# Filling rows of the sorted token table: nine scatters behind each region's last row, spread over the program, in place of three plain stores early in it

## The chip, the core and the metric

The kernel runs on one core of a Trainium2 chip. The metric is the device time of one execution in microseconds (us), as the median of several runs. TensorE is called PE here (its weight loads PEld), VectorE DVE, ScalarE ACT, GpSimd POOL, and SyncE SP. SP issues nearly all plain transfers, POOL issues the transfers whose row addresses are computed on the chip (scatters).

## The reference

A retention layer feeds a mixture of experts, and every token goes to one expert.

```python
for t in range(S):                       # B 4, H 8, S 768, D 64
    state = gamma * state + k[:, :, t] (outer) v[:, :, t]
    y[:, :, t] = scale * q[:, :, t] @ state
x = y as rows of N = 3072 tokens, 512 wide
expert_idx = argmax(x @ w_gate);  gate_w = softmax weight of that expert
for e in range(8):                       # w1 512 x 1024, w2 1024 x 512
    out[mask_e] = gate_w[mask_e] * (relu(x[mask_e] @ w1[e]) @ w2[e])
```

## The kernel before

**Retention.** The sequence is cut into 24 chunks of 128 tokens (6 for each of 4 batches), and the loop `for g in range(NCH)` handles one chunk g per step. `load(g)` brings 1 MB of q, k, v of a chunk (tiles `qkv_t`, `qkv_w`), issued by SP in the order of the program. In step g PE computes the scores of chunk g + 1 (`scores`, L256, into `sp`), the part carried from the state (L285), the transposed rows of chunk g - 1 (L314, into `tr`), the state's update (L271) and the output (L295, into `Y`). DVE masks the scores (`Sb`, L259), and `sp` has two buffers, so the scores of a chunk wait until DVE has masked those of the chunk before. POOL scales v two chunks ahead (`scale`, `vs`, L245). ACT copies rows to `xrow` (L315). Between these steps stand pieces of the first expert's weights: ACT rounds a raw piece (`whi`, L136) and POOL takes the remainder (`wlo`, L137).

**Sorting.** After each group of 6 chunks DVE picks the expert of each token (`choose`, L360 to L372, up to step g = 6 for the first group), PE ranks the tokens, and POOL scatters each chunk's 128 rows of 520 floats (`send_rows`, L629) into the table `x_sorted` in DRAM. That table has nine regions of 3200 rows: expert 0 has two (region 0 for the first half of the tokens, region 8 for the second), experts 1 to 7 one each. `KEY` is the row of each token, `cnt` the number of rows in each region.

**Reading the table.** The experts' token counts are not known ahead, so every region is read to a fixed length: 256 rows of regions 0 and 8, and `CAPS` (452, 424, ... 360) rows, rounded up to a multiple of 32, of the others, which are taken in the order of their counts (`expert_at[1]` is the expert with the most tokens; SP reads these numbers into registers at L568). What is computed from rows behind a region's last row is thrown away when the results are scattered.

**Filling rows.** `prefill` puts finite numbers into rows that a region may not reach: rows 320 to 479 of regions 1 to 7 and rows 128 to 255 of regions 0 and 8, as three plain stores (L230) that SP issues behind the load of chunk 6. Their source is the first tile of q.

**Order and waits.** The order of every engine's instructions is the order of the program text (`manual_schedule`). Waits are put in by a dependency tracker: a read of `x_sorted` waits for the scatters and stores into it that come before it in the program, a scatter waits for the reads that come before it, and scatters don't wait for one another (`scatter_rows` declares that). A new tile on old memory waits for the old tile's users.

**From the last chunk to the first experts.** After step 23 POOL scatters chunks 22 and 23. SP fetches region 8 (`xg1` and `meta8`, L147, L151), then reads the experts' numbers, then fetches region `expert_at[1]` into `buf` (L147), and then the first two pieces of that expert's w1 (`raw`, L128). PE meanwhile finishes the first half of expert 0 (L671, L688) and starts on its second half: 8 blocks of the hidden layer (L804, `ph`, three buffers), and then L827. For each block ACT writes `hh` (L809) and DVE `hl` (L810), which frees `ph`. Behind block 2 and block 3 ACT and DVE each get one half of the split of expert 1's first w1 piece (`whi`, `wlo`). `send` (L695) scatters the finished rows `yo` of expert 0's first half to `out`, in two parts.

Of the kernel before, what the change touches and what calls it, by code (L numbers as in the profile page):

```python
# [9 lines left out]
F32 = mybir.dt.float32  # L10
F32R = mybir.dt.float32r
BF16 = mybir.dt.bfloat16
I32 = mybir.dt.int32
AF = mybir.ActivationFunctionType
ALU = mybir.AluOpType
AX = mybir.AxisListType

B, H, S, D = 4, 8, 768, 64
E, DM, F = 8, 512, 1024
N = B * S  # L20
P = 128
# [10 lines left out]
E1 = E - 1  # L32
E9 = E + 1
# [5 lines left out]
REG = N + P  # L39
SLICE = P + 2  # L40
ROW = 4 * SLICE
# [57 lines left out]
def retention_moe(ctx, tc, qkv, wg, w1, w2, cst, gdec, ustr, out):  # L99
    nc = tc.nc  # L100
# [5 lines left out]
    k_ = lambda name: cs[:, OFF[name][0]:OFF[name][1]]  # L106
# [5 lines left out]
    x_sorted = tc.dram_tile([E9, REG, ROW], F32, name="x_sorted")  # L112
    x_rows = x_sorted.rearrange("e n m -> (e n) m")
# [17 lines left out]
    def split(pos, part, i, engine, n=2):  # L131
        if i == 0:
            wparts[pos, part] = [wp.tile([P, 4, 512], F32R, name=n, tag="w", bufs=11) for n in ("whi", "wlo")]
        raw, (hi, lo) = raws[pos, part], wparts[pos, part]
        h = slice(n * i, n * i + n)
        nc.scalar.copy(out=hi[:, h], in_=raw[:, h])  # L136
        engine.tensor_tensor(out=lo[:, h], in0=raw[:, h], in1=hi[:, h].bitcast(F32), op=ALU.subtract)  # L137
# [20 lines left out]
    gate = pool("gate", 1)  # L158
# [7 lines left out]
    cnt = gate.tile([P, E9], F32, name="cnt")  # L166
    capv = gate.tile([P, E9], F32, name="capv")
    cnt7 = gate.tile([P, E1], F32, name="cnt7")
    metas = {c: gate.tile([P, nb, 2], F32, name=f"meta{c}") for c, nb in ((0, 2), (E, 2), (E1, 3))}
    masks = {c: gate.tile([P, nb], I32, name=f"mask{c}") for c, nb in ((0, 2), (E, 2), (E1, 3))}  # L170
    sidxs = {c: gate.tile([P, nb], I32, name=f"sidx{c}") for c, nb in ((0, 2), (E, 2), (E1, 3))}
# [6 lines left out]
    sel, se = [gate.tile([P, E1, E1], F32, name=n) for n in ("sel", "se")]  # L178
    us = gate.tile([P, P], BF16, name="us")

    s7 = lambda t: t.unsqueeze(1).broadcast_to([P, E1, E1])
# [17 lines left out]
    with ExitStack() as actx:  # L199
# [3 lines left out]
        gsm = apool("gsm", 1)  # L203
# [9 lines left out]
        qs, vss, Sbs, xTs, lgs, Ys, xrows = {}, {}, {}, {}, {}, {}, {}  # L213
# [4 lines left out]
        def load(g, part=slice(0, 4)):  # L218
            if g not in qs:
                early = AHEAD <= g < FIRST  # L220
                qs[g] = (wp.tile([P, 4, DM], F32, name="qkv_w", tag="w", bufs=11) if early else
                         ld.tile([P, 4, DM], F32, name="qkv_t", tag="ld"))
            nc.sync.dma_start(out=qs[g][:, part], in_=qkv[g][:, part])

        def prefill():

            row = qs[0].rearrange("p i m -> p (i m)")[:, 0:ROW].unsqueeze(1)
            for classes, a, n in ((slice(1, E), 320, P), (slice(1, E), 320 + P, 32), (slice(0, E9, E), P, P)):
                dst = x_sorted[classes, a:a + n].rearrange("e n m -> n e m")
                nc.sync.dma_start(out=dst, in_=row[0:n].broadcast_to(list(dst.shape)))  # L230

        def turned(g, i):
            return qs[g][:, i].rearrange("a (p t) -> a p t", p=NP)
# [84 lines left out]
        def send_rows(g):  # L318
            b, c = divmod(g, CPB)
            scatter_rows(tc, x_rows, KEY[:, g, 0:1], xrows[b][:, c].rearrange("t q m -> t (q m)"), "sorted")  # L320

        def logits(t):
            ps, tag = (ps_m, "mt") if t < NCH // 2 - 1 else (ps_1, "misc")
            L = ps.tile([P, TW], F32, name="L", tag=tag)
            for p in range(NP):
                nc.tensor.matmul(out=L[32 * p:32 * p + 32, :], lhsT=wgs[:, p, :], rhs=xTs[t][:, p, :],
                                 start=True, stop=True)
            LT = wk.tile([P, TW], F32, name="LT", bufs=1)
            nc.scalar.copy(out=LT, in_=L)
            state["LT"] = LT  # L330
# [87 lines left out]
        def fill(n, lows=True):  # L418
            for i in range(state["half"], state["half"] + n):
                hidden(i // 2, i % 2)  # L420
                if i % 2 and lows:
                    low(i // 2, nc.gpsimd)
            state["half"] += n
# [18 lines left out]
        nc.sync.dma_start(out=us32, in_=ustr)  # L442
        for g in range(3, FIRST):
            load(g)
            if g == 6:
                prefill()
            if g in (7, 10):
                fetch(0, (g - 7) // 3)
        scores(0)
# [11 lines left out]
        for g in range(NCH):  # L461
            b, c = divmod(g, CPB)
            t = g // 2
            if LATE + 1 < g < NCH - 1:
                scores(g + 1)
            if g < NCH - 1:
                carry(g)
            if g > 0:
                rows(g - 1)
            if g + 2 < NCH:  # L470
                scale(g + 2)
            if g in placed:
                s = stages[placed[g]]
                for name in ("slots", "weights", "advance", "label"):
                    s[name]()
                if g == NCH // 2 + 2:
                    s["counts"]()
            for i in range(*sends.get(g, (0, 0))):
                send_rows(i)
            for i in splits.get(g, ()):  # L480
                split(0, *i, nc.gpsimd, 1)
            if g in logits_at:
                logits(logits_at[g])
            if g == 21:
                prep_slices(nc, nc.gpsimd, xhl[:, 0], xhl[:, 1], xt0, xg0, 0, P)
            if c < CPB - 1:
                update(g)
            if g == 21:
                prep_slices(nc, nc.gpsimd, xhl[:, 0], xhl[:, 1], xt0, xg0, 4, P)
            if g == LATE + 1:  # L490
                scores(g + 1)
            if g == NCH - 1:
                token_mask(0, cnt[:, 0:1], EARLY)
                token_index(0)
                hidden, low, result, send = early_half(tc, ld.tile([P, 2, DM], F32, name="yo0", tag="ld"),
                                            wk.tile([P, 4, EARLY], F32, name="rx0", tag="xT"),
                                            wp, ps_m, wparts, xhl, sidxs[0], metas[0], out)
                stages[3]["rank"]()
                fill(FILL[0])
                carry(g)  # L500
            output(g)
            if g in ranked and g < NCH - 1:
                stages[ranked[g]]["rank"]()
            if g <= LATE:
                scores(g + 1)
            if g == 2:
                nc.vector.tensor_copy(out=us, in_=us32)
                nc.vector.tensor_scalar(out=run, in0=k_("ebase"), scalar1=1.0 / P, scalar2=None, op0=ALU.mult)
                nc.vector.tensor_copy(out=wgs[:, :, E:E + 1], in_=wgs[:, :, 0:1])
            if g in chosen:  # L510
                s = stages[chosen[g]] = gating(chosen[g])
                s["choose"]()
                s["soft"]()
            if g == 17:
                xg0 = rawp.tile([P, NJ0, SLICE], F32, name="xg0", tag="raw")
                xt0 = rawp.tile([P, KD, EARLY], F32, name="xt0", tag="raw")
                xhl = new_xhl()
            if g < AHEAD:
                load(FIRST + g)
            elif FIRST <= g < NCH - AHEAD:  # L520
                load(g + AHEAD)
            if g == 18:
                fetch_rows(xg0, 0, NJ0)
                fetch_meta(metas[0], 0, 2)
            if g in fetches:
                fetch(0, fetches[g])
# [17 lines left out]
            final[name]()  # L544
        for g in range(22, 24):
            send_rows(g)
        fill(FILL[4])
        xg1 = ld.tile([P, NJ0, SLICE], F32, name="xg1", tag="ld")
        xt1 = ld.tile([P, KD, EARLY], F32, name="xt1", tag="ld")
# [8 lines left out]
                                       op0=ALU.mult, op1=ALU.add)  # L558
        gt = sq("gt")
        nc.vector.tensor_tensor(out=gt, in0=s7(c8), in1=i7(c8), op=ALU.is_gt)  # L560
        pos = gsm.tile([P, E1], F32, name="pos")
# [6 lines left out]
            expert_at[i + 1] = nc.sync.value_load(eid7[0:1, i:i + 1], min_val=1, max_val=E - 1)  # L568
        for f in range(done, KF):
            low(f, nc.vector)  # L570
        xg = buf[:, 0:MAXB * SLICE].rearrange("p (j m) -> p j m", m=SLICE)
        fetch_rows(xg, expert_at[1], -(-CAPS[1] // 32))
        fetch(1, 0)
# [8 lines left out]
        for j, w in pieces:  # L582
            cut_slices(nc, nc.vector, xhl1[:, 0], xhl1[:, 1], xt1, j, w)
        result(1, 0)
        result(1, 1)
        send(1)
        token_mask(E, cnt[:, E:E9], EARLY)
        token_index(E)
# [6 lines left out]
                                in1=cnt7.unsqueeze(2).broadcast_to([P, E1, 16]), op=ALU.is_ge)  # L595
        nc.vector.tensor_scalar(out=mask7, in0=empty, scalar1=float(BIG), scalar2=k_("quad"),
                                op0=ALU.mult, op1=ALU.add)
# [30 lines left out]
def scatter_rows(tc, dst, index, rows, group):  # L628
    sc = tc.nc.gpsimd.indirect_dma_start(  # L629
        out=dst, out_offset=bass.IndirectOffsetOnAxis(ap=index, axis=0),  # L630
        in_=rows, in_offset=None, bounds_check=dst.shape[0] - 1, oob_is_err=False)
    tc.declare_no_dep(sc.ins, group=group, reason="every token has one slot: the scattered rows are disjoint")
    tc.add_to_no_dep_group(group, sc.ins)
# [338 lines left out]
```

## Time and profile before

| | us |
|---|---|
| median of 3 runs | 436.0 (435.85 to 436.67) |
| profiled execution, its own time | 433.15 |
| its span in the trace | 431.4 |
| PE busy | 400.7 (93%) |
| DVE, POOL, ACT busy | 243.9, 183.9, 142.5 |
| moved by DMA | 82.65 MB |

The profiled execution is one run, 2.85 us under the median of the three, and 1.75 us of its time lie outside the span. Changes are worked out in the span and carried over to the median. In a timeline row the first number is the start, the second the duration, and the brackets tell how long the engine had been idle and what ended that.

### The profile page before, as it was taken

Reading aid. Unit: us, or ns where it says so; the run is one execution under the profiler, and the core shown is the slowest. Engines: PE = TensorE matmul, PEld = TensorE weight load, DVE = VectorE, ACT = ScalarE, POOL = GpSimd, SP = SyncE. Lnnn points to the kernel's source line nnn. Section 1 sums busy time; section 2 is a strip of 40 time slices with the busy share of each in tenths; the row PEclk is TensorE's granted clock in tenths of the full one; section 3 lists DMA queues with packets and bytes.
Section 4 is the critical chain, followed back from the end, with each engine's and each line's share of the span. In section 5 each row is a group of like instructions: output and inputs, shape, how many; then the busy total and the mean of one; then the engine's idle time right before and its main releaser. Section 6 shows DMA issues by size and latency. Waiting matters only on the chain. (4 is left out here: it accounts for less than half of the span.)

```text
span 431.4 us, 8197 instructions
## 1 busy us (share of the span) xinstructions
PE 400.7 (93%) x3271; PEld 361.3 (84%) x3271; DVE 243.9 (57%) x445; ACT 142.5 (33%) x246; POOL 183.9 (43%) x169
## 2 busy tenths in 40 slices
PE   6997889899899999999999999999999999999960
PEld 3775667677688988999999999999999999999740
DVE  1445846648652656666377477657747747746110
ACT  1122323343333254542344054235324325423000
POOL 2622776866853105000068138308506805715520
PEclk9899999999999999999999999999999999999995
DMA  7999999399333867632746454376465564600110
GB/s 266 411 382 415 410 421 381 114 352 259 126 119 107 187 235 187 226 108 88 179 150 222 86 210 156 112 171 234 148 157 180 186 138 159 237 8 31 38 60 8
DMA packets 43592, 82.65 MB, mean 192 GB/s; under 512 B 5050, under 2 KB 19262, under 8 KB 40736
## 3 DMA queue, kind: packets, MB, share of 16 engines
q1 hardware_dynamic: 38512, 69.42, 49.3%
q0 software_dynamic: 5040, 12.69, 8.0%
q8 instruction: 26, 0.43, 0.4%
q14 instruction: 14, 0.11, 0.1%
HBM read 66.55 MB, written 16.28 MB: 192 GB/s over the span
## 5 line engine op out<-in xcount | busy, mean ns | idle before, releaser
L629 POOL DMA_INDIRECT out<-Z,sidx x80 | 93.7, 1172 | 141.0 <-DVE Z L757 118.4
L137 DVE TENSOR_TENSOR wlo<-raw,whi 128x1024 fp32r<-128x1024 f32 x56 | 67.9, 1215 | 12.2 <-ACT whi L136 11.1
L136 ACT CAST whi<-raw 128x1024 fp32r<-128x1024 f32 (+1 forms) x72 | 67.2, 949 | 4.3 <-DMA raw<-w 4.0
L829 PE MATMUL py<-hh,wlo 128*128 128x452 f32 (+5 forms) x192 | 67.1, 350 | 0.0
L829 PE MATMUL py<-hl,whi 128*128 128x452 f32 (+5 forms) x192 | 66.9, 349 | 0.0
L829 PE MATMUL py<-hh,whi 128*128 128x452 f32 (+5 forms) x192 | 66.8, 348 | 0.0
L809 ACT ACTIVATE hh<-ph 128x256 fp32r<-128x256 f32 (+7 forms) x64 | 31.4, 492 | 100.1 <-PE ph L804 90.5
L810 DVE SCALAR_TENSOR_TENSOR hl<-ph,hh 128x256 fp32r<-128x256 f32 (+7 forms) x64 | 35.4, 555 | 40.0 <-ACT hh L809 35.8
L804 PE MATMUL ph<-xh,wlo 128*128 128x452 f32 (+6 forms) x224 | 50.1, 345 | 0.0
L804 PE MATMUL ph<-xl,whi 128*128 128x452 f32 (+6 forms) x224 | 50.1, 345 | 0.0
L804 PE MATMUL ph<-xh,whi 128*128 128x452 f32 (+6 forms) x224 | 50.0, 345 | 0.0
L804 PEld LDWEIGHTS ph<-xh,wlo 128*128 128x128 f32 x224 | 40.7, 188 | 0.8
L804 PEld LDWEIGHTS ph<-xh,whi 128*128 128x128 f32 x224 | 40.7, 188 | 0.8
L804 PEld LDWEIGHTS ph<-xl,whi 128*128 128x128 f32 x224 | 40.7, 188 | 0.8
L259 DVE TENSOR_TENSOR Sb<-sp,cs 128x512 f32<-128x512 f32 x48 | 30.9, 684 | 16.8 <-PE sp L256 16.7
L829 PEld LDWEIGHTS py<-hh,whi 128*128 128x128 f32 x192 | 36.0, 188 | 0.8
L829 PEld LDWEIGHTS py<-hh,wlo 128*128 128x128 f32 x192 | 36.0, 188 | 0.8
L829 PEld LDWEIGHTS py<-hl,whi 128*128 128x128 f32 x192 | 36.1, 188 | 0.7
L648 ACT CAST xh<-buf 128x512 fp32r<-128x512 f32 (+7 forms) x26 | 14.4, 556 | 59.6 <-DVE buf L639 52.2
L315 ACT COPY xrow<-tr 128x512 f32<-128x512 f32 x24 | 14.1, 586 | 56.1 <-PE tr L314 50.0
L752 DVE STREAM_TRANSPOSE Z<-py 128x416 f32<-128x416 f32 (+3 forms) x24 | 15.0, 627 | 26.9 <-PE py L829 25.9
L629 POOL DMA_INDIRECT x_sorted<-xrow,KEY x24 | 23.9, 995 | 10.8 <-DVE xrow L412 5.3
(125 smaller groups left out, 564.5 us busy)
## 6 DMA issues: line engine op xcount, KB each, us to landing
raw<-w SPq DMA_DIRECT2D x32, 1024.0 KB, 7.0
qkv_t<-qkv SPq DMA_DIRECT2D x11, 1024.0 KB, 23.2
qkv_w<-qkv SPq DMA_DIRECT2D x11, 1024.0 KB, 14.3
buf<-x_sorted SPq DMA_DIRECT2D x12, 211.2 KB, 5.1
qkv_t<-qkv SPq DMA_DIRECT2D x4, 512.0 KB, 8.0
x_sorted<-qkv_t SPq DMA_DIRECT2D x1, 1820.0 KB
buf<-x_sorted SPq DMA_DIRECT2D x8, 195.0 KB, 4.9
out<-Z,sidx POOLq DMA_INDIRECT x80
```

The source lines that it names most:

```text
L136: nc.scalar.copy(out=hi[:, h], in_=raw[:, h])
L137: engine.tensor_tensor(out=lo[:, h], in0=raw[:, h], in1=hi[:, h].bitcast(F32), op=ALU.subtract)
L259: nc.vector.tensor_tensor(out=Sb[:, r], in0=sps[r], in1=causal.unsqueeze(1).broadcast_to([P, NP, C]), op=ALU.mult)
L315: nc.scalar.copy(out=xrows[b][:, c, :, 0:P].rearrange("t q (k r) -> t q k r", r=32), in_=tr.rearrange("t k (q r) -> t q k r", r=32))
L629: sc = tc.nc.gpsimd.indirect_dma_start(out=dst, out_offset=bass.IndirectOffsetOnAxis(ap=index, axis=0), in_=rows, in_offset=None, bounds_c ...
L648: nc.scalar.copy(out=xh[:, :, sl], in_=src)
L752: nc.vector.transpose(out=Zs[e][:, 0:nb, k, :], in_=py[:, 0:32 * nb].rearrange("p (j c) -> p j c", c=32))
L804: nc.tensor.matmul(out=ph[:, :cap], lhsT=wparts[e, f // 4][a][:, kd, fo:fo + P], rhs=x[:, kd, :cap], start=(n == 0), stop=(n == 3 * KD - 1))
L809: nc.scalar.activation(out=hh[:, :cap], in_=ph[:, :cap], func=AF.Relu)
L810: nc.vector.scalar_tensor_tensor(out=hl[:, :cap], in0=ph[:, :cap], scalar=0.0, in1=hh[:, :cap].bitcast(F32), op0=ALU.max, op1=ALU.subtract)
L829: nc.tensor.matmul(out=py[:, :cap], lhsT=a[:, f % 4, k * P:(k + 1) * P], rhs=x[:, :cap], **se)
```

## The change

`prefill` and its call are removed. A new tile `pads` holds, for each region, 128 row numbers: the region's first row plus its count plus 0 to 127. `pad_rows` computes them on DVE, and `send_pad` scatters 128 rows there, with `xrow` rows of finished chunks as the source. So the 128 rows behind each region's last row are filled. The nine scatters stand at four places: region 0 in step 16; region 8 behind the scatters of chunks 22 and 23; the region of `expert_at[1]` behind the last `low`, ahead of its fetch; and the six others, in the order of the experts, between the two parts of `send`. For experts 1 to 7 four small DVE instructions bring the counts into that order.

```diff
-        def prefill():
-            row = qs[0].rearrange("p i m -> p (i m)")[:, 0:ROW].unsqueeze(1)
-            for classes, a, n in ((slice(1, E), 320, P), (slice(1, E), 320 + P, 32), (slice(0, E9, E), P, P)):
-                dst = x_sorted[classes, a:a + n].rearrange("e n m -> n e m")
-                nc.sync.dma_start(out=dst, in_=row[0:n].broadcast_to(list(dst.shape)))
...
+        def pad_rows(which, count, first):
+            nc.vector.tensor_scalar(out=pads[:, which], in0=count, scalar1=k_("pos")[:, 0:1], scalar2=first,
+                                    op0=ALU.add, op1=ALU.add)
+
+        def send_pad(i, x):
+            scatter_rows(tc, x_rows, pads[:, i:i + 1], x.rearrange("t q m -> t (q m)"), "sorted")
...
-            if g == 6:
-                prefill()
...
+            if g == 16:
+                pad_rows(slice(0, 1), cnt[:, 0:1], 0.0)
+                send_pad(0, xrows[1][:, 0])
...
         for g in range(22, 24):
             send_rows(g)
+        pad_rows(slice(E, E9), cnt[:, E:E9], float(REG * E))
+        send_pad(E, xrows[3][:, 0])
...
         for f in range(done, KF):
             low(f, nc.vector)
+        ends = gsm.tile([P, E1], F32, name="ends")
+        nc.vector.tensor_tensor(out=ends, in0=cnt[:, 1:E], in1=k_("ebase")[:, 1:E], op=ALU.add)
+        nc.vector.tensor_tensor(out=gt, in0=sel, in1=s7(ends), op=ALU.mult)
+        nc.vector.tensor_reduce(out=ends, in_=gt, axis=AX.X, op=ALU.add)
+        pad_rows(slice(1, E), ends, 0.0)
+        send_pad(1, xrows[3][:, 0])
         xg = buf[:, 0:MAXB * SLICE].rearrange("p (j m) -> p j m", m=SLICE)
         fetch_rows(xg, expert_at[1], -(-CAPS[1] // 32))
...
         result(1, 0)
         result(1, 1)
+        for i in range(2, E):
+            send_pad(i, xrows[3][:, 0])
         send(1)
```

On PE and ACT no instruction is added, taken away or moved. SP, in the first 25 us, before the change (`qkv_w` are chunk loads 4 and later, `raw` the first weight piece):

```order
L223 DMA qkv_t<-qkv 128x2048
L223 DMA qkv_w<-qkv 128x2048 x3
L230 DMA x_sorted<-qkv_t 128x7x520
L230 DMA x_sorted<-qkv_t 32x7x520
L230 DMA x_sorted<-qkv_t 128x2x520
L223 DMA qkv_w<-qkv 128x2048
L128 DMA raw<-w 128x4x512
L223 DMA qkv_w<-qkv 128x2048 x3
```

The same place after the change:

```order
L224 DMA qkv_t<-qkv 128x2048
L224 DMA qkv_w<-qkv 128x2048 x4
L128 DMA raw<-w 128x4x512
L224 DMA qkv_w<-qkv 128x2048 x3
L128 DMA raw<-w 128x4x512
```

The three stores are gone, and the load of chunk 7 follows that of chunk 6 directly. POOL, from the scatters of chunks 18 to 21 to the second half of expert 0, before the change (`yo` are finished rows of expert 0, `xl` is expert 1's input):

```order
L629 DMA x_sorted<-xrow,KEY 28800x520 x4
L679 TENSOR_TENSOR hl_1647<-rx_1645,hh_1646 128x256
L629 DMA x_sorted<-xrow,KEY 28800x520 x2
L679 TENSOR_TENSOR hl_1647<-rx_1645,hh_1646 128x256 x2
L629 DMA out<-yo_1644,sidx_87 3072x512 x2
L649 TENSOR_TENSOR xl<-buf,xh 128x4x128 x3
L629 DMA out<-yo,sidx_88 3072x512 x2
```

The same place after the change:

```order
L642 DMA x_sorted<-xrow,KEY 28800x520 x4
L692 TENSOR_TENSOR hl_1649<-rx_1647,hh_1648 128x256
L642 DMA x_sorted<-xrow,KEY 28800x520 x2
L642 DMA x_sorted<-xrow,pads 28800x520
L692 TENSOR_TENSOR hl_1649<-rx_1647,hh_1648 128x256 x2
L642 DMA x_sorted<-xrow,pads 28800x520
L642 DMA out<-yo_1646,sidx_88 3072x512
L642 DMA x_sorted<-xrow,pads 28800x520 x6
L642 DMA out<-yo_1646,sidx_88 3072x512
L662 TENSOR_TENSOR xl<-buf,xh 128x4x128 x3
```

Eight of the nine filling scatters (`pads`) stand here: one ahead of the last two `hl`, one ahead of the first scatter of `yo`, and six between the two scatters of `yo`. By the tracker's waits, the second of the eight waits for the fetches of `xg1` and `meta8`, SP's fetch of `buf` waits for that second one to land, and the third waits for the fetch of `buf` to land. The tile `xl` now lies on the memory of `yo`, so that it also waits for the two scatters of `yo`.

## Rows read from the trace of the kernel before

**Rows 1.** The page's first part: busy time of an engine, its share of the span, and its instructions.

```profile
PE 400.7 (93%) x3271; PEld 361.3 (84%) x3271; DVE 243.9 (57%) x445; ACT 142.5 (33%) x246; POOL 183.9 (43%) x169
```

**Rows 2.** Busy time by stretch: from and to, length, busy us of PE, PEld, DVE, ACT and POOL (with instructions), and at the end PE's granted clock, the share of time that the 16 DMA engines were busy, and GB/s.

```profile
10.00:36.00 26.00, 23.87 (x374) 18.89 (x371) 12.32 (x23) 5.43 (x12) 10.36 (x11) 0.94 1.03 398
36.00:47.00 11.00, 8.66 (x139) 6.80 (x139) 7.33 (x12) 3.20 (x8) 5.55 (x5) 1.00 1.03 413
...
143.50:149.50 6.00, 6.00 (x43) 5.57 (x42) 3.74 (x18) 0.77 (x2) 0.98 (x1) 1.00 1.10 233
149.50:154.50 5.00, 5.00 (x43) 4.95 (x42) 1.50 (x4) 2.25 (x4) 0.00 (x0) 1.00 1.04 386
```

**Rows 3.** Timeline of PE in the chunk loop: the output of chunk 5, and the scores of chunks 7, 8 and 9.

```profile
33.34 1.09 PE L295 MATMUL Y<-Sb,vs 128*64 128x128 f32 x16
...
36.25 1.16 PE L256 MATMUL sp<-qkv_w 64*128 64x128 f32 x16 [1.82 <-DMA qkv_w<-qkv]
...
41.44 1.16 PE L256 MATMUL sp<-qkv_w 64*128 64x128 f32 x16 [0.66 <-DMA qkv_w<-qkv]
...
46.69 1.75 PE L256 MATMUL sp<-qkv_w 64*128 64x128 f32 x16 [1.15 <-DVE Sb L259]
```

**Rows 4.** Timeline of SP (SPq: its queue, where the duration is the time of issuing): the three stores, and the load behind them.

```profile
12.22 9.92 SPq L230 DMA_DIRECT2D x_sorted<-qkv_t  x3
22.18 1.23 SPq L223 DMA_DIRECT2D qkv_w<-qkv  x1
```

**Rows 5.** The page's sixth part: transfers issued, KB each, and where it is known the median us from issue to landing.

```profile
x_sorted<-qkv_t SPq DMA_DIRECT2D x1, 1820.0 KB
...
xg<-x_sorted SPq DMA_DIRECT2D x8, 130.0 KB, 3.1
...
x_sorted<-qkv_t SPq DMA_DIRECT2D x1, 520.0 KB
x_sorted<-qkv_t SPq DMA_DIRECT2D x1, 455.0 KB
```

**Rows 6.** Timeline of DVE and POOL while the first group's experts are chosen (L360 to L372), and last the same instruction as L363 for a later group.

```profile
36.27 1.04 POOL L245 TENSOR_TENSOR vs<-qkv_w,cs 128x512 f32<-128x512 f32 x1 [9.03 <-DMA qkv_w<-qkv]
...
41.46 1.04 POOL L245 TENSOR_TENSOR vs<-qkv_w,cs 128x512 f32<-128x512 f32 x1 [4.15 <-DMA qkv_w<-qkv]
41.55 0.19 DVE L360 TENSOR_REDUCE mx<-lg 128x6 f32<-128x48 f32 x1
...
42.47 2.51 POOL L137 TENSOR_TENSOR wlo<-raw,whi 128x512 fp32r<-128x512 f32 x2
42.60 1.20 DVE L363 TENSOR_TENSOR eq<-eq,cs 128x48 f32<-128x48 f32 x1
...
44.96 1.08 DVE L372 TENSOR_TENSOR sh<-lg,mx 128x48 f32<-128x48 f32 x1
45.96 1.27 DVE L259 TENSOR_TENSOR Sb<-sp,cs 128x512 f32<-128x512 f32 x2
...
116.92 0.19 DVE L363 TENSOR_TENSOR eq<-eq,cs 128x32 f32<-128x32 f32 x1
```

**Rows 7.** Who waited for whom on SP's queue: us in total, times, longest.

```profile
SPq L147 <- DMA x_sorted<-xrow,KEY: 34.0, 1, 34.0
```

**Rows 8.** Timeline of POOL, DVE and SP from the last scatter into the table to the fetch of expert 1's first weights.

```profile
130.62 0.98 POOL L629 DMA_INDIRECT x_sorted<-xrow,KEY  x1 [0.30 <-issue]
...
134.67 1.80 SPq L147 DMA_DIRECT2D xg<-x_sorted  x4
...
136.52 0.45 SPq L151 DMA_DIRECT2D meta<-x_sorted  x1
...
140.62 0.75 DVE L692 TENSOR_SCALAR yo<-py,meta 128x512 f32<-128x512 f32 x1 [4.13 <-PE py L688]
...
141.65 0.99 POOL L629 DMA_INDIRECT out<-yo,sidx  x1 [8.61 <-DVE yo L692]
...
141.94 2.07 SPq L147 DMA_DIRECT2D buf<-x_sorted  x4
...
144.19 12.68 SPq L128 DMA_DIRECT2D raw<-w  x3
...
147.09 0.98 POOL L629 DMA_INDIRECT out<-yo,sidx  x1 [4.44 <-DVE m L190]
```

**Rows 9.** Timeline of ACT, DVE and PE in the second half of expert 0, where expert 1's first weights come in.

```profile
152.64 1.05 ACT L136 CAST whi<-raw 128x1024 fp32r<-128x1024 f32 x1 [1.88 <-DMA raw<-w]
153.59 0.38 ACT L809 ACTIVATE hh<-ph 128x256 fp32r<-128x256 f32 x1
...
154.92 0.42 DVE L810 SCALAR_TENSOR_TENSOR hl<-ph,hh 128x256 fp32r<-128x256 f32 x1
...
155.39 0.74 PE L804 MATMUL ph<-xhl,whi 128*128 128x256 f32 x4 [0.74 <-DVE hl L810]
```

**Rows 10.** Timeline of POOL: two places where it stood idle.

```profile
91.18 1.04 POOL L245 TENSOR_TENSOR vs<-qkv_t,cs 128x512 f32<-128x512 f32 x1 [1.95 <-DMA qkv_t<-qkv]
...
163.94 2.14 POOL L649 TENSOR_TENSOR xl<-buf,xh 128x512 fp32r<-128x512 f32 x2 [15.87 <-issue]
```

**Rows 11.** Busy time by stretch, as in rows 2, in the experts' part.

```profile
165.00:255.00 90.00, 90.00 (x453) 84.55 (x452) 57.10 (x86) 34.35 (x49) 23.31 (x21) 1.00 0.54 157
255.00:345.00 90.00, 90.00 (x494) 89.82 (x493) 59.43 (x89) 36.11 (x52) 47.21 (x40) 1.00 0.56 175
```

More of the change, by code (lines that the diff above doesn't have):

```diff
@@ L168, in retention_moe @@
     cnt7 = gate.tile([P, E1], F32, name="cnt7")
+    pads = gate.tile([P, E9], I32, name="pads")
     metas = {c: gate.tile([P, nb, 2], F32, name=f"meta{c}") for c, nb in ((0, 2), (E, 2), (E1, 3))}
```

## The prediction

> **What bounds the kernel now.** I read the busy times first: PE is busy for 93% of the span [rows 1], and in the experts' part it works without a gap (90.00 of 90.00 us, twice) [rows 11]. So whatever shifts PE's work ahead of 165 us shifts the end by as much. Second, the stretches of the chunk loop: from 10 to 47 us the DMA engines are full (share 1.03, about 400 GB/s), and PE is busy for only 8.66 of 11.00 us from 36 to 47 us [rows 2]. Third, PE's own waits there: chunk 7's scores wait 1.82 us for the chunk's load, chunk 8's wait 0.66 us, and chunk 9's wait 1.15 us for DVE's mask [rows 3]. Fourth, the hand-over to the experts: SP, POOL, ACT and PE from 130 to 156 us [rows 7 to 9]. There a chain of transfers ends in a wait of PE (0.74 us at 155.39), so it has no slack at its end.
>
> **What is removed.** The three stores move 1820 + 520 + 455 = 2795 KB, that is 2.86 MB [rows 5], in the same queue as the chunk loads and ahead of chunk 7 [rows 4]. At 398 GB/s [rows 2] this is 7.2 us of full DMA time. Everything queued behind lands that much earlier: chunk 7 at about 36.25 - 7.2 = 29.0 us, chunk 8 at 34.2. PE is ready for chunk 7 at 34.43 (33.34 + 1.09) [rows 3], and then for chunk 8 at about 38.9. So both loads come some 5 us before they are wanted, and the waits of 1.82 + 0.66 = 2.48 us go. What is late next is DVE's mask of chunk 8, behind the choice of experts. That choice took from 41.55 to 45.96 us, and its instructions are long while POOL computes beside them: L363 took 1.20 us beside POOL's `wlo`, and 0.19 us for a later group (32 elements against 48) without it [rows 6]. POOL was there because its scaling had waited 9.03 and 4.15 us for the same two loads [rows 6]. With the loads early POOL does this work some 4 us sooner, most of it is over when the choice starts, and the 1.15 us of chunk 9 go too. **Gain: 1.82 + 0.66 + 1.15 = 3.6 us.** Bounds: at least 1.8 us, if the choice stays as long and only the first wait comes out of its chain; at most 4.2 us, if chunk 9's scores also take 1.16 us like others, not 1.75 [rows 3].
> The Trainium skill (GPSIMD Engine Reference, Key points) says that POOL shares its SBUF interfaces with DVE and contends with DVE instructions that have two SBUF inputs. Rows 6 agree (1.20 against 0.19 us). By that rule the gain would be the 3.6 us, and without it the 1.8.
>
> **What is added, place by place.** A scatter takes POOL 0.98 us plus 0.30 us of issue, 1.28 in all, and SP, which waited for the scatters before [rows 7], went on 134.67 - 130.62 = 4.05 us after the last one's start [rows 8]. I take 4.05 us from start to landing. The six small DVE instructions are like the 0.19 us of rows 6; the four for experts 1 to 7 fall into the 4.13 us in which DVE stood idle ahead of `yo` at 140.62 [rows 8], the other two cost at most 0.4 us of a DVE that nobody waits for there: nothing.
> Region 0, step 16: POOL stood idle for 1.95 us ahead of 91.18, behind that step's scatters [rows 10], and 1.28 us fit: nothing. Without that cover it would be 1.28 us of POOL, two chunks ahead of PE's need.
> Region 8: SP's fetch of `xg1` moves from 134.67 to 135.95. The fetches take 3.1 us [rows 5], so the last lands at about 140.9 where DVE starts to turn the tile behind `yo` (140.62 + 0.75 = 141.4): just covered, 0 to 0.5 us, I take 0.
> Region of `expert_at[1]`: this is the dear one. SP's `meta8` is issued by 136.97 + 1.28 = 138.25, and it lands about 3 us after that at most (the nearest row is that of `xg`) [rows 5], near 141.1. Only then may POOL scatter (a write behind reads), and it lands at 145.15. SP's fetch of `buf`, which started at 141.94 [rows 8], waits for it: **3.2 us late**. Behind it on SP stand the first weights of expert 1 (144.19) [rows 8]. They are already late in the kernel before: ACT waits 1.88 us for them at 152.64, and as ACT works in order, `hh` (153.59), `hl` (154.92) and PE (155.39) follow [rows 9]. So each us by which these weights land later is one us of PE.
> Part of it comes back. The fetch of `buf` and the weights move at the full DMA share (1.10 and 1.04) [rows 2], and in that stretch the two scatters of `yo` move as well, 256 KB each (128 rows of 512 floats). After the change the first goes out ahead of the late fetch, and the second only behind six fillings, after these weights. 0.52 MB at 386 GB/s [rows 2] are about 1.3 us. **Cost: 3.2 - 1.3 = 1.9 us.** Bounds: 0.8, if `meta8` lands a us sooner; 4.2, if nothing comes back and the fillings take one us of DMA time from the weights.
> Regions of the other six: POOL starts them when `buf` has landed, at about 151.5, and is done by 151.5 + 6 x 1.28 = 159.2. POOL stood idle for 15.87 us ahead of `xl` at 163.94 [rows 10], which itself moves back with PE. The second scatter of `yo` (147.09 before) [rows 8] goes out at about 159.5 and lands near 163.6, ahead of `xl` at 165.8, which now waits for it: nothing, with 2 us to spare; if that cover went, expert 1's start would slip by what is over.
>
> **The sum.** -3.6 + 1.9 = -1.7 us on the profiled execution, 433.15 to 431.45. That execution lies 2.85 us under the median of 436.0; the difference carries over: **434.3 us**.
>
> **Rivals.**
> *The choice stays slow* (same). If DVE's long instructions don't depend on POOL, or POOL's work lands on them again, the gain is 1.8 and the cost 1.9 to 2.5: 435.9 to 436.7. For it: DVE needs 4.4 us for six small instructions, and only L363 has a counterpart. Against it: that counterpart, six times shorter.
> *The fillings take the weights' bandwidth* (slower). Six scatters of 266 KB, one each 1.28 us, ask for 208 of 386 GB/s. If they start while about half of the first 1 MB weight piece (1.2 us of it) is still to move, that rest runs at 178 GB/s and takes 2.6 us: +1.4 us; if the fillings meet the whole piece, +3.2 us. With the second and nothing back from `yo`, the cost is 3.2 + 3.2 = 6.4 us less the gain of 3.6: +2.8, 438.8 us; with the middle, 3.2 + 1.4 = 4.6, +1.0, 437.0 us. The point from which it decides is a cost of 3.6 us. Against it: the fillings wait until `buf` has landed, and the weights have been moving since its last bytes left.
> The Trainium skill (DMA: Bandwidth & Descriptors, SWDGE vs HWDGE vs iDMA) says that the DMA engines take turns between the queue that POOL feeds and the others. No row here shows a scatter beside such a load alone. By this rule the scatters get their 208 GB/s, and only their start decides.
> *The chain is shorter* (faster still). If `meta8` and the filling land faster, the weights are under 1 us late, and with the gain of 4.2 this is 432.5 us.
> *It doesn't do what it says*: the loads are held by something else than the stores. Against it: the share of 1.03 [rows 2]. It would leave the cost alone, 437.9 us.
>
> **How the numbers follow.** Forecast (433.2 to 435.2) 0.53, choice stays slow 0.23, bandwidth rival 0.11, shorter chain 0.10, stores not the reason 0.03. A measurement of this kernel tells about 0.2% (0.87 us) from no change: faster is under 435.1, slower over 436.9. Faster: nearly all of the forecast (0.50) and the shorter chain (0.10), 0.60. Same: the slow choice, the rest of the forecast, and the mild end of the bandwidth rival, 0.28. Slower: the rest, 0.12. The range goes from the shorter chain's 432.4 to the bandwidth rival's mild end, 437.0, which leaves out about a tenth on top and a few in a hundred below.
>
> **What would show it.** In the new trace: chunks 7 and 8 without a wait for DMA, the choice in under 3 us, and chunk 9's scores at about 43.1 us; POOL's filling for region 0 in the idle gap; SP's fetch of `buf` about 3 us later against PE's L688; ACT's wait for the first weights 1.88 + 1.9 = 3.8 us, and PE's wait in L804 0.74 + 1.9 = 2.6 us. Wrong would be the forecast if PE's wait there is over 4 us, if PE gets a new wait at the start of expert 1 (for `xl`), or if the chunk loop is not at least 2 us shorter.

## The result, and the profile after

| | before | after |
|---|---|---|
| median of 4 runs | 435.93 us (434.62 to 436.67) | 423.75 us (423.60 to 424.48) |
| profiled execution, its span | 433.15, 431.4 | 423.78, 421.9 |
| PE's last matmul ends | 417.3 | 416.3 |
| last scatter of the program ends | 419.4 | 418.4 |

The ratio is 0.9727, 95% interval 0.9701 to 0.9753: 12.2 us faster, and outside the range predicted. Here and below a time is the median of all runs, while a ratio leaves out runs more than 1.5% above the fastest of their kernel, so it is not quite the quotient of two medians. The last two lines of the table tell where to look: up to the last scatter the changed kernel is only 1.0 us ahead, and 8.4 us lie behind it, where no engine computes.

The difference (after less before, us) along the program, from PE's starts in the two timelines:

| chunk 9 scores | chunk 16 scores | chunk 19 scores | expert 0, first half | expert 1 | PE's end | end of span |
|---|---|---|---|---|---|---|
| -3.54 | -4.95 | -3.35 | -2.90 | -1.84 | -0.99 | -9.44 |

First the page's busy times, and the stretches of the chunk loop (columns as in [rows 2]), of the changed kernel:

```profile
PE 401.4 (95%) x3271; PEld 361.7 (86%) x3271; DVE 242.7 (58%) x451; ACT 142.0 (34%) x246; POOL 191.7 (45%) x178
```

```profile
10.00:36.00 26.00, 26.00 (x394) 20.75 (x390) 12.57 (x23) 5.54 (x12) 12.05 (x12) 0.91 1.01 410
36.00:47.00 11.00, 11.00 (x191) 8.45 (x189) 8.41 (x19) 5.19 (x13) 7.28 (x7) 1.00 1.02 413
```

PE works the 11.00 us from 36 to 47 without a gap, where it was busy for 8.66 [rows 2]; the queue is as full as before. PE's scores of chunks 7, 8 and 9, and then DVE's choice of experts, in the timeline of the changed kernel (no brackets: no wait):

```profile
35.01 1.16 PE L250 MATMUL sp<-qkv_w 64*128 64x128 f32 x16
...
39.12 1.16 PE L250 MATMUL sp<-qkv_w 64*128 64x128 f32 x16
...
43.15 1.40 PE L250 MATMUL sp<-qkv_w 64*128 64x128 f32 x16
```

```profile
39.97 0.19 DVE L362 TENSOR_REDUCE mx<-lg 128x6 f32<-128x48 f32 x1
...
41.94 0.20 DVE L374 TENSOR_TENSOR sh<-lg,mx 128x48 f32<-128x48 f32 x1
```

The three waits of [rows 3] are gone, and the choice takes 2.2 us where it took 4.4 [rows 6].

Then a place of the kernel before that the prediction did not look at: ACT splits the third piece of expert 0's weights behind a wait for its load, and PE waits for ACT's next instruction, `ub`. Timelines of ACT and of PE before:

```profile
75.32 1.14 ACT L136 CAST whi<-raw 128x512 fp32r<-128x512 f32 x2 [1.42 <-DMA raw<-w]
```

```profile
76.78 0.67 PE L285 MATMUL Y<-qkv_w,ub 64*64 64x128 f32 x16 [1.33 <-ACT ub L274]
```

and of the changed kernel, where neither waits:

```profile
69.94 1.14 ACT L136 CAST whi<-raw 128x512 fp32r<-128x512 f32 x2
```

```profile
71.52 0.67 PE L279 MATMUL Y<-qkv_w,ub 64*64 64x128 f32 x16
```

Behind the scatter for region 0 the changed kernel loses time. Its timelines of POOL, DVE and PE at chunk 18:

```profile
84.82 0.97 POOL L642 DMA_INDIRECT x_sorted<-xrow,pads  x1 [0.30 <-issue]
```

```profile
86.57 0.23 DVE L344 TENSOR_REDUCE lg<-lp 128x16 f32<-128x64 f32 x1 [3.67 <-PE sp L250]
```

```profile
83.54 0.44 PE L340 MATMUL lp<-cs,LT 128*128 128x128 f32 x2
...
87.54 0.67 PE L279 MATMUL Y<-qkv_t,ub 64*64 64x128 f32 x16 [2.47 <-DVE xT L297]
```

DVE needs `lp`, which is done at 83.98, and starts at 86.57. The hand-over (as [rows 8, 9]), timelines of POOL, SP, ACT and PE:

```profile
137.74 0.99 POOL L642 DMA_INDIRECT x_sorted<-xrow,pads  x1 [6.06 <-DMA meta<-x_sorted]
```

```profile
140.66 2.18 SPq L147 DMA_DIRECT2D buf<-x_sorted  x4
143.03 18.49 SPq L128 DMA_DIRECT2D raw<-w  x4
```

```profile
150.70 1.05 ACT L136 CAST whi<-raw 128x1024 fp32r<-128x1024 f32 x1 [1.97 <-DMA raw<-w]
```

```profile
153.45 0.74 PE L817 MATMUL ph<-xhl,whi 128*128 128x256 f32 x4 [0.83 <-DVE wlo L137]
```

L688 (L701 in the changed kernel) is the last part of PE's work on expert 0's first half. Its first row, before and after:

```profile
134.95 0.40 PE L688 MATMUL py<-whi,hh 128*128 128x512 f32 x1
```

```profile
132.92 0.40 PE L701 MATMUL py<-whi,hh 128*128 128x512 f32 x1
```

SP's fetch of `buf` is 1.28 us earlier than before while PE's L688 is 2.03 earlier, so the fetch is 0.75 us late against PE; PE's wait is 0.83 us where it was 0.74 [rows 9].

Last the end of the program. The rows are groups of instructions of one source line: POOL's queue issues its last two kinds behind the last scatter (durations in ns as min/median/max, then the start of the first and of the last). Before:

```profile
L616 POOLq INC_SWDGE_SEM  x1: 2390/2390/2390, 419.0 to 419.0; - x1
```

```profile
L968 POOLq DRAIN  x3: 40/107/9130, 421.4 to 431.1; - x3
```

and after:

```profile
L629 POOLq INC_SWDGE_SEM  x1: 438/438/438, 418.0 to 418.0; - x1
```

```profile
L981 POOLq DRAIN  x3: 40/107/2641, 418.5 to 421.7; - x3
```

I call these two, from the last scatter's end to the end of the span, **the closing**: 431.38 - 419.44 = 11.9 us before, 421.94 - 418.44 = 3.5 after. INC_SWDGE_SEM belongs to the branch that leaves out `moe_rest`, and the DRAIN to the end of the program; the long one of the three DRAINs is the first.

### The profile page after: what moved, and what is told of

Read it like the earlier page. It is cut to its first block, busy times and chain, and to the rows that moved or that the text cites. A ratio compares the mean times of both kernels' runs of the same rounds, so it can differ in the third digit from the quotient of the medians.

```text
span 421.9 us, 8222 instructions
## 1 busy us (share of the span) xinstructions
PE 401.4 (95%) x3271; PEld 361.7 (86%) x3271; DVE 242.7 (58%) x451; ACT 142.0 (34%) x246; POOL 191.7 (45%) x178
## 5 line engine op out<-in xcount | busy, mean ns | idle before, releaser
L642 POOL DMA_INDIRECT out<-Z,sidx x80 | 92.1, 1151 | 142.5 <-DVE Z L770 119.9
```

The lines of the kernel that those rows point to most:

```text
L642: sc = tc.nc.gpsimd.indirect_dma_start(out=dst, out_offset=bass.IndirectOffsetOnAxis(ap=index, axis=0), in_=rows, in_offset=None, bounds_c ...
```

## The experiments

**What sets the closing.** Theory "number": the count of scatters issued (111 before, 120 after). Rival "stores": the plain stores. In each kernel the line numbers shift a little.

*stores_back*: the changed kernel and the early stores.

```diff
...
+            if g == 6:
+                prefill()
```

> The changed kernel with the three early stores put back behind the load of chunk 6: 120 scatters and the stores. In the traces so far POOL's last piece of work behind its last scatter (its closing DRAIN) took 9.13 us before the change and 2.64 us after it. Theory 'number': its length goes with the number of scatters that POOL has issued (111 before, 120 after), or with which of the eight completion semaphores, taken in turn, is next. Then it stays near 2.6 us here, and only the chunk loop goes back: PE reaches the first half of expert 0 about 2.9 us later than in the changed kernel, and the time is 423.8 + 2.9 = about 426.7 us. Rival 'stores': the plain stores make the closing long. Then it is near 9 us and the time about 433 to 435 us.

Closing 0.44 + 2.64 us (INC_SWDGE_SEM, then the first DRAIN), as in the changed kernel: the stores are not its cause. 430.88 us (425.5 to 433.67), ratio to the kernel before 0.9891 (0.9852 to 0.9930). That is 4 us more than expected. Its profiled execution, one of its longer ones at 432.68 us, loses time in the chunk loop: chunk 16 begins at 84.5 us, against 75.4 in the changed kernel and 80.4 before.

*one_filling*: the kernel before and the scatter for region 0.

```diff
...
+            if g == 16:
+                pad_rows(slice(0, 1), cnt[:, 0:1], 0.0)
+                send_pad(0, xrows[1][:, 0])
```

> The kernel before, with one scatter of the change added, that of region 0 in step 16: 112 scatters, the early stores stay. Theory 'number', by the semaphore that is next (112 and 120 are both multiples of eight): the closing is near 2.6 us, and the time some 8 us under that of the kernel before, about 427 us. By the sheer number (a count that has to be passed somewhere between 111 and 120) it is open. Rival 'stores': closing near 9 us, the time that of the kernel before, about 436 us.

436.74 us, ratio 1.0051 (1.0014 to 1.0087). The closing is long at 112 scatters too, so the next semaphore of eight is not the cause. Its DRAIN, and at 75 to 85 us a wait as in the kernel before, but 5 us long (ACT, PE, then the stretches, columns as in [rows 2]):

```profile
L980 POOLq DRAIN  x3: 40/107/9212, 424.3 to 434.0; - x3
```

```profile
77.06 1.14 ACT L136 CAST whi<-raw 128x512 fp32r<-128x512 f32 x2 [5.11 <-DMA raw<-w]
```

```profile
78.53 1.13 PE L286 MATMUL Y<-qkv_w,ub 64*64 64x128 f32 x16 [5.02 <-ACT ub L275]
```

```profile
75.00:80.00 5.00, 1.48 (x18) 1.15 (x19) 0.98 (x8) 1.41 (x3) 2.24 (x2) 0.61 0.24 93
80.00:85.00 5.00, 5.00 (x62) 3.52 (x60) 0.79 (x2) 1.33 (x3) 4.28 (x5) 0.70 0.27 107
```

PE idles, and its granted clock falls from 1.00 (2.4 GHz, in the 5 us ahead of these) towards 0.5 (1.2 GHz): 0.61 and then 0.70 on average, while PE is busy for all of the second stretch.

*eight_fillings*: the changed kernel without the scatter for region 0; those rows come from one small early store.

```diff
-                send_pad(0, xrows[1][:, 0])
...
+            nc.sync.dma_start(out=x_sorted[0:1, P:2 * P].rearrange("e n m -> n e m"), in_=row)
```

> The changed kernel without the scatter for region 0: 119 scatters. The rows 128 to 255 of that region are filled instead by one plain store of 260 KB behind the load of chunk 6. Theory 'number' by the semaphore that is next (119 as 111 is one short of a multiple of eight): the closing is near 9 us, the time about 423.8 + 8 = 432 us. By a count passed between 111 and 120: near 2.6 us and 423 to 424 us. Rival 'stores': with a small store left, anything between, most likely near 2.6 us. The chunk loop should gain up to 2 us at chunks 18 and 19 if the scatter for region 0 held POOL there.

419.88 us, ratio 0.9674 (0.9626 to 0.9723), closing 0.43 + 2.64 us at 119 scatters, so the next semaphore does not decide. Chunk 18 to 19 takes 3.30 us, against 5.84 in the changed kernel, and the time is 3 to 4 us under the 423 to 424 us expected for a short closing.

*stores_late*: the stores moved to step 11, their source a finished row of `xrow`.

> The kernel before, with the three stores moved from behind the load of chunk 6 to step 11, ahead of the last piece of expert 0's weights: 111 scatters, all of the stores, no scatter added. The chunk loop should lose its waits as in the changed kernel (chunk 9's scores at about 43 us against 46.7), and the hand-over to the experts none of the time that the filling scatters cost, so PE should end 3 to 4 us earlier than in the kernel before. Theory 'number': the closing stays near 9 us, the time is about 432 us. Rival 'stores' (only early ones lengthen the closing): near 2.6 us, about 424 us.

435.45 us, ratio 1.0029 (1.0002 to 1.0055); closing 2.39 + 9.13 us at 111, as "number" has it. Of the time this was a flawed experiment: ACT, about to overwrite that tile, waited 9.48 us for the stores to read it, and chunk 16 began at 85.3 us. Chunk 9 was at 43.9, as expected.

*spare_8, spare_30, spare_4*: the kernel before with 8, 30 or 4 scatters of constants to a scratch memory, where POOL idles.

```diff
+        for i in range(8):
+            scatter_rows(tc, scratch[i], spot, cs[:, 0:DM], "spare")
```

> The kernel before, untouched but for eight extra scatters (and one small DVE instruction for their row numbers) at about 172 to 182 us, where POOL has nothing to do; they write constants to a scratch memory that nobody reads. 119 scatters, as in eight_fillings. If the number of scatters alone sets the closing, POOL's last DRAIN is near 2.6 us instead of 9.1, and the time is that of the kernel before less 8.5 us, about 425 us. If something else of the change does it (where the scatters stand, the removed stores), it stays at 9.1 us and 434 us.

427.19 us, ratio 0.9827 (0.9766 to 0.9888), with nothing but idle work added:

```profile
L973 POOLq DRAIN  x3: 40/107/2596, 422.7 to 426.0; - x3
```

> The same with thirty extra scatters, 172 to 211 us: 141 scatters. If the closing is short from some count on, the last DRAIN is near 2.6 us. If its length grows by some 0.08 us with each scatter since a point that lies between 112 and 119 (9.13 us at 111, 9.21 at 112), it is 1.8 to 2.4 us longer than at 119, some 4.4 to 5.0 us.

0.87 + 2.92 us: longer than at 119, less than expected.

> The same with four extra scatters: 115 scatters. It halves the interval between 112 (9.21 us) and 119 (2.64 us). Either near 2.6 us (the point lies between 112 and 115), or near 9.45 us (0.08 us for each scatter over 111; the point lies between 115 and 119).

0.34 + 2.55 us: the point lies between 112 and 115.

*spare_60, spare_119*: the same, to tell a threshold from a count that begins anew.

> The kernel before with sixty extra scatters from 172 us on: 171 scatters; they hold up POOL's own work behind them, so only the closing is read. If its length goes with the scatters since a point that comes at about every 114th, 57 stand behind it: by the slopes so far (INC_SWDGE_SEM 0.34 us at 115, 0.43 at 119, 0.87 at 141; DRAIN 2.92 at 141, 9.13 at 111) about 1.4 us for the first and 5 us for the second. If the closing is just short above 114, 0.4 and 2.6 us, as at 119; spare_30 would then be a stray.

```profile
L621 POOLq INC_SWDGE_SEM  x1: 1469/1469/1469, 476.5 to 476.5; - x1
```

```profile
L973 POOLq DRAIN  x3: 40/107/5373, 478.0 to 483.9; - x3
```

> The same with 119 extra scatters: 230 in all. If the point comes again at twice the count, 226 to 230 (between 113 and 115 the first time), the closing is short again, near 0.4 and 2.6 us. If it came only once, 116 scatters stand behind it, and the closing is long, 2.5 and over 9 us.

```profile
L973 POOLq DRAIN  x3: 40/107/2761, 566.6 to 569.9; - x3
```

Both came as the count that begins anew has it. (What these two take in all, 486 and 572 us, is their own load on POOL.)

**How the gain divides.** *late_111, early_115, late_115*: early or late stores by 111 or 115 scatters, on one chip with the kernel before. The late stores now read a tile of constants, and no filling scatter is in any of them.

```diff
-            if g == 6:
-                prefill()
...
+            if g == 11:
+                prefill()
```

> The kernel before with its three stores moved to step 11 and fed from a tile of constants: late stores, 111 scatters, no filling scatter. The closing should be the long one (12 us from the last scatter to the end of the span). If the early stores cost 5 to 10 us by the chunk loop alone, the ratio to the kernel before is 0.977 to 0.988.

> spare_4 again: early stores, 115 scatters. The closing is short, the chunk loop as in the kernel before: 8.4 us less than the kernel before, ratio about 0.981.

> stores_late_4 again: late stores, 115 scatters. If the two parts add, its gain is that of late_111 and that of early_115 together, a ratio of 0.953 as on the last chip, 0.958 to 0.969 by the bounds of the two; if it is clearly less or more than their sum, they touch the same time or help each other.

| us (ratio to the kernel before, interval) | 111 scatters | 115 scatters |
|---|---|---|
| early stores | 434.69 (the kernel before) | 426.60 (0.983, 0.976 to 0.990) |
| late stores | 428.01 (0.9842, 0.9800 to 0.9884) | 421.52 (0.9685, 0.9645 to 0.9726) |

The count is worth 8.1 us beside early stores and 6.5 beside late ones, the early stores 6.7 and 5.1; together they are worth 13.2, a little less than the sum of 14.8. The last kernel of the table has no filling at all, and it is about as fast as a variant of the changed kernel on the same chip (*pads_15* below, 423.67 us). *stores_late_4*, the lower right kernel on another chip:

> The kernel before with two things changed. The three stores go from behind the load of chunk 6 to step 11 as in stores_late, but from a tile of constants that nobody overwrites, so ACT needs not wait for them (in stores_late it waited 9.48 us for the stores to read its rows); and four idle scatters are added as in spare_4, so that 115 scatters are issued. No filling scatter. If the early stores cost the chunk loop all that the changed kernel gained there, and the count of scatters the rest, this has both gains and no dearer hand-over: PE at chunk 16 at about 74 us (73.9 in eight_fillings, 80.4 to 85.7 in the kernels with the early stores), closing 3.6 us behind the last scatter, 416.5 to 418.5 us in all. If the late stores hold the first group's second half of scatters or the last weight piece, PE waits at chunks 15 to 18, and the time is 420 us or more.

420.65 us beside 441.96 of the kernel before there, 0.953 (0.947 to 0.959). Chunk 16 began at 74.6 us, as expected, but the time lies above the 416.5 to 418.5 us. The same program as late_115 has ratios of 0.953 and 0.9685 on two chips, so differences of 1% between ratios from different chips say little.

**The loss at chunk 18.** *after_again* is the changed kernel; *pads_15* computes the row numbers for region 0 in step 15; *scatter_17* issues its scatter in step 17.

> The changed kernel itself, profiled once more. In its first trace DVE stood idle for 3.67 us at chunk 18, 2.5 us of them behind the matmul that it waited for, and ACT for 5.89 us ahead of its last instruction of the last expert; PE lost 2.5 and 0.95 us by these. Neither wait shows its end. If the program makes them, they are there again; if they belong to that execution, they are gone, and the span is some 3 us shorter.

Both waits are there again: DVE 3.70 us, ACT 8.07 us. DVE's belongs to the program. ACT's comes back with another length, and PE lost 3.97 us by it where it had lost 0.96.

> The changed kernel, with the row numbers for region 0 computed one step earlier on DVE (step 15); its scatter stays in step 16. If DVE's idle 2.6 us behind the logits' matmul at chunk 18 hang on the instruction just ahead of it, they go, and PE reaches chunk 19 about 2.5 us earlier (chunk 18 to 19 in 3.3 us, not 5.84). If they hang on the scatter, or on neither, they stay.

423.67 us, ratio 0.9737 (0.9696 to 0.9778). The wait stays (DVE 3.81 us).

> The changed kernel with the scatter for region 0 moved from step 16 to step 17, where POOL issues it behind the scaling of v for a chunk instead of straight behind two other scatters. If DVE's idle 2.6 us at chunk 18 hang on that scatter's place, chunk 18 to 19 takes about 3.3 us instead of 5.84, and the wait is gone or stands one chunk later. If it stays at chunk 18 with the same length, the scatter is not its cause.

DVE stands 1.2 us behind `lp` where it stood 2.6, and chunk 18 to 19 takes 4.43 us: the scatter's place matters, but does not explain all of it. In these four traces DVE starts 0.64 to 0.86 us behind the end of POOL's run of scatters (85.79 and 86.57 us in the changed kernel), whether the run ends with the filling or, as in scatter_17, with a scatter of a chunk. But it need not wait for such a run. In one_filling and stores_back the same scatter stands in step 16, and chunk 18 to 19 takes 3.30 us in both. POOL and DVE there, in one_filling, whose `lp` is done at 92.64:

```profile
91.88 0.97 POOL L641 DMA_INDIRECT x_sorted<-xrow,pads  x1 [0.30 <-issue]
```

```profile
92.68 0.22 DVE L351 TENSOR_REDUCE lg<-lp 128x16 f32<-128x64 f32 x1 [2.21 <-PE lp L347]
```

DVE starts while the scatter still runs. And late_111, which has no filling, shows a like wait one chunk earlier: DVE starts `xT` at 79.94 us, 1.5 us behind its input and 0.55 behind two scatters of POOL, and PE waits 1.23 us for it. So the wait goes with runs of POOL's scatters in some traces and not in others; what decides is open.

**A kernel that may be better still.** *seven_fillings*: eight_fillings, and region 8 filled by the same early store. It issues 118 scatters.

> eight_fillings, with the rows 128 to 255 of region 8 filled by the same small early store (520 KB in all for regions 0 and 8) instead of a scatter behind those of chunks 22 and 23: 118 scatters, seven of them fillings. SP's fetch of region 8 starts one scatter, about 1.28 us, earlier against PE, and with it the whole hand-over: PE's wait in the second half of expert 0 gets shorter, and the time is 0.5 to 1.3 us under that of eight_fillings (ratio about 0.965). If the early store of 520 KB pushes chunk 7 or the last weight piece into PE's way, or if 118 is short of the count from which the closing is short, it is slower than eight_fillings (by up to 2, or by 9 us).

418.38 us, ratio 0.9631 (0.9577 to 0.9685). From expert 0's first half to expert 1 it takes 51.2 us, against 52.6 in eight_fillings: the scatter for region 8 was on the path of the hand-over. About half of the 1.4 us lies ahead of L688 (15.91 us from the first half's start, against 16.66), and eight_fillings shows how; POOL, ACT and PE there:

```profile
125.32 1.14 POOL L645 DMA_INDIRECT x_sorted<-xrow,pads  x1 [0.30 <-issue]
126.46 1.43 POOL L695 TENSOR_TENSOR hl<-rx,hh 128x256 fp32r<-128x256 f32 x2
```

```profile
127.25 0.38 ACT L691 ACTIVATE rx<-ph 128x256 f32<-128x256 f32 x1 [2.10 <-POOL hl L695]
```

```profile
127.69 0.50 PE L704 MATMUL py<-whi,hh 128*128 128x512 f32 x1 [0.58 <-ACT rx L691]
```

The scatter stands ahead of POOL's last two `hl`, ACT's `rx` waits for the buffer that `hl` reads, and PE waits for `rx`. Whether seven_fillings is faster than eight_fillings or the changed kernel is not shown: the three were timed on different chips, and the intervals of the first two overlap (0.9577 to 0.9685, 0.9626 to 0.9723).

## Why the prediction was wrong, point by point

**The first two waits, the mask, the choice** (3.6 us of gain): right, 3.54 us at chunk 9, whose scores start at 43.15 us (43.1 predicted). The changed kernel's execution was already 0.65 us behind at chunk 6 (31.71 against 31.06), whose load goes ahead of the stores; over all runs that start lies between 30.8 and 32.8 us. From chunk 6 on the gain is 4.2 us, the prediction's upper bound.

**What else queues behind the stores**: the term was too small. The prediction said that everything queued behind lands earlier, and then followed chunks 7 and 8 alone. The third weight piece lies in that queue too; PE waited 1.33 us for it in the trace shown, and 0.6 to 5.0 us in the profiles of other kernels with early stores. Behind the waits of 2.15 to 5.02 us (spare_60, spare_4, stores_back, spare_8, spare_119, spare_30, one_filling) the granted clock fell. In the profiled pair the lead at chunk 16 is 4.95 us; the table above puts the early stores at 5.1 to 6.7 us, against the 3.6 of the prediction. That is also the likely reason why the medians differ by 12.2 us and the spans by 9.4: the profiled execution of the kernel before, with 1.33 us, was 2.8 us under its median. Its other executions left no trace, so this is argued, not shown.

**Region 0 "in POOL's idle 1.95 us: nothing"**: wrong in the changed kernel, where PE loses 2.47 us at chunk 18 (0.51 before; in the pair the lead shrinks by 2.0 us from chunk 18 to 19). POOL's time was free, as the prediction said; DVE's was not. In stores_back and one_filling the same scatter costs nothing there. What ends DVE's wait is in no row, and it stays open.

**Region 8 "just covered"**: not as free as taken; by seven_fillings against eight_fillings about 1.4 us of the hand-over. The prediction followed the fetch of `xg1` alone, not POOL's `hl` behind the scatter. The changed kernel has the same wait of PE, and is 0.87 us slower than the kernel before from the first half's start to L688 (18.07 against 17.20):

```profile
131.38 0.51 PE L684 MATMUL ph<-xhl,whi 128*128 128x256 f32 x2 [0.53 <-ACT rx L688]
```

A like wait of 0.60 us stands in stores_late_4, which has no filling, so the size there is not the scatter's alone.

**Region of `expert_at[1]`** (1.9 us of cost, 0.8 to 4.2): the path was right, the size too large. The filling landed 140.66 - 137.74 = 2.9 us behind its start, not 4.05; against L688 `buf` is 0.75 us late, not 3.2; ACT waits 1.97 us, not 3.8, and PE 0.83, not 2.6. The hand-over from expert 0's first half to expert 1 costs 52.80 - 51.74 = 1.06 us in the pair, but only 34.73 - 34.54 = 0.2 of it lies behind L688, which is under the bounds. In seven_fillings, without region 8's scatter, that part costs 0.75 us (35.29), in eight_fillings 1.4 (35.90). (Two small slips: by the prediction's own figures `meta8` lands at 138.25 + 3.1 = 141.35, not 141.1, and the rival of the slow choice begins at 436.1 us, not 435.9.)

**The other six: nothing**: right. The second scatter of `yo` went out at 156.96, and POOL's `xl` at 162.71 waited for ACT alone. The first weights came 150.70 - 143.03 = 7.7 us behind the start of their issue, 8.5 before [rows 8, 9], so the rival of the bandwidth fell; so did the slow choice and "it doesn't do what it says".

**The sum**: here the prediction failed. It let the end of the span follow PE, with all behind PE's end unchanged. The parts up to PE's end come to -0.99 us in the pair (-1.7 predicted); the closing, in none of the terms, gives 8.4 of the 9.44 us. spare_8 shows that it is the count: eight scatters that do nothing useful make the kernel before 6.5 us faster in the median. By stores_back, stores_late and the table of four kernels, the stores and the fillings' places have no part in it. Every scatter here has 128 rows of about 2 KB, so no run tells the count of scatters from the count of rows or bytes. The 11.9 us stood in the trace before, as the stretch from the last scatter to the end of the span.

PE lost another 0.96 us at 404 us, where ACT's `hh` came late in the last expert (5.89 us of idle, 8.07 in after_again; 3.81 in the kernel before, where PE did not wait); why is open.

## What to carry to other kernels

Look at what fills the time from the last useful instruction to the end of the span, and at what it counts: here the number of scatters decides on 8 us that no engine's busy time shows. When bytes leave a full queue, follow every transfer that waits in it, to the last one that an engine waits for, not only the next two. Filler work placed in one engine's idle time is free only if nothing behind it on that engine, and no other engine, turns out to wait there.

## What was not expected of the hardware

**POOL's closing goes with the scatters since a point that comes again.** By number of scatters, durations in us:

| scatters | 111 | 112 | 115 | 118 | 119 | 120 | 141 | 171 | 230 |
|---|---|---|---|---|---|---|---|---|---|
| INC_SWDGE_SEM | 2.39 | 2.40 | 0.34 | 0.40 | 0.43 | 0.44 | 0.87 | 1.47 | 0.52 |
| first DRAIN | 9.13 | 9.21 | 2.52 to 2.56 | 2.60 | 2.60 to 2.64 | 2.63 to 2.67 | 2.92 | 5.37 | 2.76 |

From 115 to 171 the first grows by 1.13 / 56 = 0.020 us per scatter, from 141 to 171 the second by 2.45 / 30 = 0.082, and between 112 and 115, and again between 171 and 230, both fall back. From 115 to 141 the DRAIN grows by less than 0.4 us in all; the filling of 137.74 needed up to 2.9 us to land, and if the last scatter needs as long, that may be why. By the slope of 0.020 the 0.52 us at 230 stand some 9 scatters further behind their point than the 0.34 at 115 behind theirs, so the second point is known only to lie between 171 and 230. One could read this as a list of fixed length that POOL's transfers fill and that is worked through at the end; the runs show the count only. The Trainium skill (DMA: Bandwidth & Descriptors, SWDGE vs HWDGE vs iDMA) says that POOL's software appends the descriptors of its transfers to rings; no run here shows such a ring.

**A stall of PE costs more than its length.** In one_filling the 5.0 us of waiting were followed by the low clock shown above, and from chunk 15 to 16 it took 12.35 us; in stores_back, with 2.52 us of waiting and a granted clock of 0.71 and 0.60 from 75 to 80 and 80 to 85 us, 10.38. The changed kernel, which does not wait there, takes 5.60 us: 6.75 and 4.78 us less. In the kernel before, 1.33 us of waiting left the clock at 1.00, and it took 6.69 us.
